# Reordering the turn into the gated MLP: tile 4's attention ahead of the transposes of tiles 0 and 1, tile 3 turned next to tile 2

## The chip, the cores and the metric

The kernel runs on one core of one Trainium2 chip. A core has five engines that run their own instruction queues: TensorE (PE, matrix products, with the loading of weights shown apart as PEld), VectorE (DVE), ScalarE (ACT), GpSimd (POOL) and SyncE (SP), which issues most of the DMA transfers. They meet by semaphores. The metric is device time in microseconds; before the change the median of four runs is 825.15 us (824.64 to 827.29).

## The reference

The program computes the output and the gradients of one transformer layer with S = 2048 rows, D = 640 columns and 32 heads of 20, followed by a gated MLP of width F = 1728. Cut to what matters:

```
phi(t) = where(t > 0, t + 1, exp(t)) + 1e-6
A(x):  q, k, v = heads of x @ wqkv
       kv = phi(k).T @ v ; z = sum of phi(k)          # per head
       o  = (phi(q) @ kv) / (phi(q) . z + 1e-6)
       return o @ wo
B(x):  return (silu(x @ w1) * (x @ w3)) @ w2

h   = x + A(layernorm(x))
out = h + B(layernorm(h))
returns out and, for a given grad_out, the gradients of x, wqkv, wo, w1, w3, w2
```

All inputs and outputs are bf16. The scores are never formed: the attention is linear, so that for one tile of rows it is a product of the normalised phi(q) with one matrix of 640 x 640 that holds kv and wo together (`Wp` in the kernel).

## The kernel before

Rows are worked in 16 tiles of 128 (`t`), and the MLP in four blocks of four tiles (`c`). The order of the work is written by hand: the framework keeps the order in which the program issues instructions on each engine and adds the waits, so a list of steps is the schedule. Every engine takes its own instructions strictly in that order.

The program has these stages: layer norm, q, k, v and the sums over rows for all tiles (to about 74 us); a turn into the second half of the layer (about 74 to 100 us); the forward gated MLP over four blocks with the attention of later tiles mixed in (about 100 to 344 us); then the weight and input gradients (to the end). The change is in the second of these, in the tuple of steps handed to `run` (lines 868 to 876). A step is a function with its arguments. Those that the change moves or passes are:

- `f2_half(t, j, hold)` calls `f2_at` (line 634): half `j` (320 columns) of the attention output of tile `t`, five products into a PSUM buffer named `at`, from the transposed phi(q) of the tile (`pqT`) and `Wp`. For the second halves of tiles 0 to 3 (and both of tiles 5 to 7) a sixth product with the identity adds x (line 640), and ACT copies the sum to `x_sb` (line 647); otherwise DVE adds x (line 649). Then DVE takes the statistics of the half (line 147), and after the second half their aggregate and variance (lines 150 and 153); POOL makes the reciprocal deviation `ln_rs` (line 154). With `hold` the part after the products is kept back until `f2_rest`.
- `f2_hn(t)` (line 727): the normalised rows `hn` of a tile on DVE (line 160), and a store of them issued on SP (line 732). Tiles 0 and 1 have buffers of their own. Tile 2 takes over a buffer of the group `pql`, which held scaled phi(q) of an earlier tile until its DMA transpose (line 376) and its store had read it. Tile 3 takes one of the group `h2`, which held products of tile 6 that the reduction `r_red(6, (0,))` reads.
- `f2_ht(t)` (line 734): for tiles 0 to 3, five transposes of `hn` on PE into a PSUM buffer `trh` (line 744) and one ACT copy of it into `pqT` (line 745), which is then the operand `hnT` of the MLP. For later tiles it is a DMA.
- `mlp_ghh(n)` (line 756): one product of grad_out with w2, five products on PE (line 386) and a cast on ACT (line 406). It needs none of the steps around it.
- `r_red`, `r_inv`, `r_scale`, `r_T` (lines 363 to 376): the denominators of a later tile on DVE, and its DMA transpose on SP.

`trh` and the MLP's and grad_out's products share four PSUM buffers of the group `mm` in turn. The `at` of tile 4 has two buffers of the group `o2` in turn, used before by tiles 0 and 2. The MLP (`mlp`, line 760) follows; its first product reads all four tiles of the first block at once, and so waits for the last of the four copies at line 745.

Of the kernel before, what the change touches and what calls it, by code (L numbers as in the profile page):

```python
# [9 lines left out]
P = 128  # L10
# [8 lines left out]
S, D, H, F = 2048, 640, 32, 1728  # L19
# [36 lines left out]
def kernel(  # L56
# [807 lines left out]
    def kv3():  # L864
# [5 lines left out]
        (f2_wT, 4), (phi_rest,), (q_late, 14), (r_T, 4), (load_x, 4, 6), (r_head, 5), (r_prod, 7),  # L870
        (r_store, 5, 6), (r_store, 4, 5), (f2_m_out,), (q_out, 10, 14), (load_w2T, 8 * P, 10 * P), (mlp_ghh, 4),
        (q_late, 15), (sig_table,), (f2_half, 0, 0), (f2_half, 1, 0), (f2_half, 2, 0), (f2_half, 3, 0), (mlp_ghh, 5),
        (f2_half, 0, 1), (f2_half, 1, 1), (f2_hn, 0), (f2_half, 2, 1), (f2_hn, 1), (f2_half, 3, 1), (f2_ht, 0),
        (f2_half, 4, 0, True), (load_w2T, 10 * P, F), (f2_hn, 2), (f2_ht, 1), (mlp_ghh, 6), (r_red, 6, (0,)),
        (f2_hn, 3), (r_red, 6, (1,)), (f2_ht, 2), (r_inv, 6), (r_scale, 6), (r_T, 6), (mlp_ghh, 7), (f2_ht, 3),
        (f2_half, 4, 1, True), (f2_rest,), (r_red, 7), (r_inv, 7), (r_scale, 7), (r_T, 7), (r_store, 6, 7))
    p1.release()
    pa = pool("pa", "right")

# [627 lines left out]
```

## Time and profile before

| what | us |
|---|---|
| median of 4 runs | 825.15 |
| the profiled execution | 824.92 |
| its span in the trace | 823.20 |
| PE busy | 816.7 (99%) |
| DVE busy | 453.0 (55%) |
| ACT busy | 325.2 (40%) |
| POOL busy | 133.0 (16%) |

Times in the trace count from the start of the span. An instruction's row has its start, its length, engine, line, operation, what it writes and reads, and in brackets the idle time of its engine just before it with what ended that. PE's products are pipelined: a row's length holds the depth of the pipeline, so the next row starts before the last has ended, and a short wait hides in that overlap. Around the edited steps, from 86 to 100 us, PE is busy 12.74 of 14 us, DVE 11.84, ACT 8.52 and POOL 5.36; from 100 to 200 us PE is busy all of the time.

### The profile page before, as it was taken

The numbers are of one execution on the slowest core, as the hardware profiler recorded it, in microseconds if no ns is written. First come the engines' busy times: TensorE is split into PE (matmuls) and PEld (weight loads), VectorE is DVE, ScalarE is ACT, GpSimd is POOL, SyncE is SP. The second block draws the span as 40 slices with busy tenths as digits, with TensorE's granted clock in tenths as the row PEclk, the third lists the DMA queues.
The fourth block names the chain that finished last, engine by engine and source line by source line (L and its number), as shares of the span: only waits on it lengthen the run. The fifth ranks groups of instructions, "written<-read, shape, count | busy, mean of one in ns | idle before, by whom it ended". The sixth has DMA issues, their size and how long they took to land.

```text
span 823.2 us, 14206 instructions
## 1 busy us (share of the span) xinstructions
PE 816.7 (99%) x5549; PEld 522.1 (63%) x5549; DVE 453.0 (55%) x961; ACT 325.2 (40%) x609; POOL 133.0 (16%) x194
## 2 busy tenths in 40 slices
PE   8999999999999999999999999999999999999998
PEld 6677544555555555777777777777777777555554
DVE  7868888999898566300057777772681545200000
ACT  7856688655565666011121212222212334211111
POOL 2243333233322212100001111110220000000000
PEclk9999999999999999999999999999999999999999
DMA  9999989696485556999777898358994898885771
GB/s 223 260 281 228 205 217 298 210 242 166 137 218 156 155 192 167 228 241 266 216 166 182 197 211 185 74 111 173 255 234 93 164 197 178 208 194 140 167 168 38
DMA packets 320883, 157.26 MB, mean 191 GB/s; under 512 B 238704, under 2 KB 314064, under 8 KB 320816
## 3 DMA queue, kind: packets, MB, share of 16 engines
q1 hardware_dynamic: 278768, 115.54, 61.8%
q10 hardware_dynamic: 34720, 16.34, 8.8%
q0 software_dynamic: 7328, 24.48, 8.8%
q8 instruction: 43, 0.70, 0.4%
q14 instruction: 24, 0.20, 0.1%
HBM read 47.01 MB, written 51.13 MB: 119 GB/s over the span
## 4 chain that ended last, share of the span: by engine, by line
PE 96%; DMA 1%; ACT 1%; DVE 1%; issue 0%; SPq 0%; DVEq 0%
PE mm L386 20%; PE job L1271 19%; PE ghn L1070 14%; PE gxn L1429 8%; PE o L833 7%; PE gw L1025 7%; PE big L266 4%; PE gwo L1155 3%; PE macc L416 3%; PE gr L1127 3%; PE dkv L1375 3%; PE at L642 2%; DMA pqT<-pql 1%; DMA wqkv<-in_A_wqkv_dram 1%; PE dkv L1303 1%; PE gp L386 1%
## 5 line engine op out<-in xcount | busy, mean ns | idle before, releaser
L1271 PE MATMUL job<-gb,hnN 128*128 128x432 bf16 (+2 forms) x656 | 117.0, 342 | 0.0
L1070 PEld LDWEIGHTS <-ggb 128*128 128x128 bf16 x864 | 84.4, 98 | 33.0
L1271 PEld LDWEIGHTS <-hnN 128*128 128x128 bf16 x656 | 63.5, 98 | 53.5
L386 PE MATMUL mm<-pqT,w 128*128 128x512 bf16 x405 | 93.6, 379 | 0.3 <-ACT pqT L745 0.3
L386 PEld LDWEIGHTS <-w 128*128 128x128 bf16 x540 | 52.4, 98 | 63.5 <-issue 1.3
L1275 ACT CAST obs<-job 128x432 bf16<-128x432 f32 (+3 forms) x61 | 29.3, 480 | 123.1 <-PE job L1271 123.1
L833 PE MATMUL o<-w,hhT 128*128 128x320 bf16 x448 | 67.7, 299 | 0.0
L1070 PE MATMUL ghn<-w13a,ggb 128*128 128x320 bf16 x448 | 63.5, 299 | 0.0
L1070 PE MATMUL ghn<-w13b,ggb 128*128 128x320 bf16 x416 | 61.4, 299 | 0.0
L386 PE MATMUL mm<-g2T,w2T 128*128 128x512 bf16 x240 | 59.6, 379 | 0.0
L833 PEld LDWEIGHTS <-hhT 128*128 128x128 bf16 x448 | 43.7, 98 | 23.9 <-issue 0.2
L1025 PE MATMUL gw<-g,hb 128*128 128x320 bf16 x416 | 56.8, 299 | 0.0
L1135 POOL TENSOR_TENSOR sz<-Zb,g_h 128x640 f32<-128x640 bf16 x16 | 20.2, 1261 | 198.8 <-DVE g_h L1133 198.8
L1025 PEld LDWEIGHTS <-hb 128*128 128x128 bf16 x416 | 40.5, 98 | 16.1 <-issue 0.3
L1429 PE MATMUL gxn<-wqT,gT 128*128 128x320 bf16 x320 | 48.7, 299 | 0.0
L406 ACT CAST ghh<-mm 128x512 bf16<-128x512 f32 x48 | 28.4, 592 | 44.1 <-PE mm L386 39.3
L772 ACT ACTIVATE sig<-mm 128x512 bf16<-128x512 f32 x56 | 33.7, 601 | 25.1 <-PE mm L386 21.0
L1082 ACT ACTIVATE gs<-ghn 128x640 bf16<-128x640 f32 x16 | 11.2, 703 | 79.0 <-PE ghn L1070 69.2
L386 PEld LDWEIGHTS <-w2T 128*128 128x128 bf16 x260 | 25.2, 98 | 23.6 <-DMA w2T<-in_B_w_dram 0.3
L266 PEld LDWEIGHTS <-pqT 128*128 128x128 bf16 x320 | 30.5, 97 | 14.0 <-issue 1.2
L1429 PEld LDWEIGHTS <-gT 128*128 128x128 bf16 x320 | 31.3, 98 | 12.2
L266 PE MATMUL big<-wqkv,pqT 128*128 128x320 bf16 x250 | 38.5, 299 | 0.2
(210 smaller groups left out, 1282.7 us busy)
## 6 DMA issues: line engine op xcount, KB each, us to landing
hh_d<-hhT SPq DMA_DIRECT2D x24, 256.0 KB, 2.8
gg_d<-gate POOLq DMA_DIRECT2D x24, 256.0 KB, 4.5
gg_d<-ghh POOLq DMA_DIRECT2D x24, 256.0 KB, 3.5
ggb<-gg_d SPq DMA_DIRECT2D x6, 896.0 KB, 5.5
ggb<-gg_d ACTq DMA_DIRECT2D x6, 832.0 KB, 5.9
out_dram<-obs ACTq DMA_DIRECT2D x39, 108.0 KB, 3.1
x_sb<-in_A_x_dram SPq DMA_DIRECT2D x6, 640.0 KB, 6.2
ggb<-gg_d SPq DMA_DIRECT2D x2, 1728.0 KB, 13.3
```

The source lines that it names most:

```text
L266: T.matmul(acc, lhsT=pqT[:, c, t * P:(t + 1) * P], rhs=wqkv[:, c, n0:n0 + HD], start=(c == 0), stop=(c == DT - 1))
L386: T.matmul(acc[:], lhsT=w[:, c, fc * P:(fc + 1) * P], rhs=rhs[:, c, :], start=(c == 0), stop=(c == DT - 1))
L406: A.copy(out=ghh[n // 2][:, n % 2, :], in_=acc[:])
L416: T.matmul(macc[m][j][:, 0:n], lhsT=pk_all[:, t, m * P:(m + 1) * P], rhs=x_ext[:, t, j * HD:j * HD + n], start=(t == 0), stop=(t == ST - 1))
L772: A.activation(sig[:, i, :], gp[:], AF.Sigmoid)
L833: T.matmul(o2["ps"][:, 0:HD], lhsT=hhT[c][:, fc, i * P:(i + 1) * P], rhs=w2[:, fc, j * HD:(j + 1) * HD], start=(fc == 0), stop=(fc == FT - 1))
L1025: T.matmul(acc[:, j, 0:HD], lhsT=hb[b][:, t, i * P:(i + 1) * P], rhs=g2[:, t, j * HD:(j + 1) * HD], start=(t == 0), stop=(t == ST - 1))
L1070: T.matmul(acc[:, j, 0:HD], lhsT=ggb[t // 2][:, k, lo:lo + P], rhs=rhs[:, j * HD:(j + 1) * HD], start=(k == 0), stop=(k == NG - 1))
L1127: T.matmul(gr[t][:, j, 0:HD], lhsT=ghT[t][:, c, :], rhs=wT2[:, c, j * HD:(j + 1) * HD], start=(c == 0), stop=(c == DT - 1))
L1271: T.matmul(acc[:, 0:n], lhsT=lhs[:, t, m * P:(m + 1) * P], rhs=rhs(t), start=(t == 0), stop=(t == ST - 1))
L1275: A.copy(out=ob, in_=acc[:, 0:n])
L1429: T.matmul(acc[:, j, 0:HD], lhsT=g, rhs=wqT[:, k, j * HD:(j + 1) * HD], start=(k == 0), stop=(k == 14))
```

## The change

Only the order of the steps is changed, in one tuple. Tile 4's two halves are issued ahead of the transposes of tile 0 and of tile 1; the first reduction of tile 6 is issued ahead of `hn` of tile 2, and `hn` of tile 3 sooner; the transposes of tile 3 follow those of tile 2; the last grad_out product of the stretch follows them; and the reductions and the scaling of tile 6 stand behind.

```diff
-        (f2_half, 0, 1), (f2_half, 1, 1), (f2_hn, 0), (f2_half, 2, 1), (f2_hn, 1), (f2_half, 3, 1), (f2_ht, 0),
-        (f2_half, 4, 0, True), (load_w2T, 10 * P, F), (f2_hn, 2), (f2_ht, 1), (mlp_ghh, 6), (r_red, 6, (0,)),
-        (f2_hn, 3), (r_red, 6, (1,)), (f2_ht, 2), (r_inv, 6), (r_scale, 6), (r_T, 6), (mlp_ghh, 7), (f2_ht, 3),
-        (f2_half, 4, 1, True), (f2_rest,), (r_red, 7), (r_inv, 7), (r_scale, 7), (r_T, 7), (r_store, 6, 7))
+        (f2_half, 0, 1), (f2_half, 1, 1), (f2_hn, 0), (f2_half, 2, 1), (f2_hn, 1), (f2_half, 3, 1),
+        (f2_half, 4, 0, True), (f2_ht, 0), (load_w2T, 10 * P, F), (r_red, 6, (0,)), (f2_hn, 2), (f2_half, 4, 1, True), (f2_hn, 3),
+        (f2_ht, 1), (mlp_ghh, 6), (r_red, 6, (1,)), (f2_ht, 2), (f2_ht, 3), (r_inv, 6), (r_scale, 6), (r_T, 6),
+        (mlp_ghh, 7), (f2_rest,), (r_red, 7), (r_inv, 7), (r_scale, 7), (r_T, 7), (r_store, 6, 7))
```

Engine by engine, in the order in which the instructions stand:

| engine | before | after |
|---|---|---|
| PE | tile 3's attention, turn 0, tile 4 first half, turn 1, grad_out, turn 2, grad_out, turn 3, tile 4 second half, MLP | tile 3's attention, tile 4 first half, turn 0, tile 4 second half, turn 1, grad_out, turn 2, turn 3, grad_out, MLP |
| DVE | hn 2, reduction, hn 3, reduction | reduction, hn 2, hn 3, reduction |
| ACT | copy 0, copy 1, cast, copy 2, cast, copy 3 | copy 0, copy 1, cast, copy 2, copy 3, cast |
| POOL, SP | | as before |

Here "turn" is the five transposes of a tile, "copy" the ACT copy of them, and "cast" that of a grad_out product.

## The prediction

> **What bounds the kernel now.** I read the page's busy times first, then its chain, then who made TensorE (PE) wait in the whole run, then all engines from 92 to 104 us, where the edited steps run. From the page, busy time of PE and the chain's shares by engine:
>
> ```profile
> PE 816.7 (99%) x5549; PEld 522.1 (63%) x5549; DVE 453.0 (55%) x961; ACT 325.2 (40%) x609; POOL 133.0 (16%) x194
> PE 96%; DMA 1%; ACT 1%; DVE 1%; issue 0%; SPq 0%; DVEq 0%
> ```
>
> PE sets the end. The kernel gets shorter only where PE idles, and PE's waits over the whole run make five lines, 3.1 us together. Two of them belong to the edited stretch:
>
> ```profile
> PE trh L744 <- DVE hn L160: 0.7, 2, 0.5
> ...
> PE mm L386 <- ACT pqT L745: 0.3, 1, 0.3
> ```
>
> The others lie before 91 us. So after 99.8 us nothing is shown to hold PE back, and a shift there should reach the end. The chain in order of time says what the stretch hangs on (start, length, what):
>
> ```profile
> 89.38 6.95 DMA pqT<-pql
> ...
> 96.45 0.46 DVE hn L160
> ...
> 96.95 0.45 PE trh L744 x5
> ...
> 99.01 0.71 ACT pqT L745
> ```
>
> The normalised rows hn of tile 2 take over the buffer of a pql tile, and wait for that tile's transposing DMA, issued at 89.38 and landed at 96.33. Tile 2's transposes, at 96.95, follow from that. The timeline below names POOL as releaser of that hn; but POOL's row for tile 2 ended at 95.29, the one that ended near 96.35 is tile 3's, so I go by the chain. The timeline, PE's rows first, then those of VectorE (DVE) and ScalarE (ACT); the brackets hold idle time and releaser:
>
> ```profile
> 93.76 0.45 PE L744 MATMUL trh<-ident,hn 128*128 128x128 bf16 x5 [0.22 <-DVE hn L160]
> 94.05 0.84 PE L642 MATMUL at<-Wp,pqT 128*128 128x320 bf16 x5
> 94.94 0.45 PE L744 MATMUL trh<-ident,hn 128*128 128x128 bf16 x5
> 95.23 1.24 PE L386 MATMUL mm<-g2T,w2T 128*128 128x512 bf16 x5
> 96.95 0.45 PE L744 MATMUL trh<-ident,hn 128*128 128x128 bf16 x5 [0.48 <-DVE hn L160]
> 97.25 1.24 PE L386 MATMUL mm<-g2T,w2T 128*128 128x512 bf16 x5
> 98.33 0.44 PE L744 MATMUL trh<-ident,hn 128*128 128x128 bf16 x5
> 98.60 0.84 PE L642 MATMUL at<-Wp,pqT 128*128 128x320 bf16 x5
> 99.76 8.79 PE L386 MATMUL mm<-pqT,w 128*128 128x512 bf16 x40 [0.31 <-ACT pqT L745]
> ```
>
> ```profile
> 96.45 0.45 DVE L160 TENSOR_SCALAR hn<-x_sb,ln_mv,ln_rs 128x640 bf16<-128x640 bf16 x1 [0.73 <-POOL ln_rs L154]
> 96.81 0.48 DVE L365 TENSOR_REDUCE rden<-pr 128x16 f32<-128x320 f32 x1
> 97.40 0.45 DVE L160 TENSOR_SCALAR hn<-x_sb,ln_mv,ln_rs 128x640 bf16<-128x640 bf16 x1
> ```
>
> ```profile
> 97.45 0.69 ACT L745 COPY pqT<-trh 128x640 bf16<-128x640 bf16 x1 [0.35 <-PE trh L744]
> 98.53 0.59 ACT L406 CAST ghh<-mm 128x512 bf16<-128x512 f32 x1 [0.39 <-PE mm L386]
> 99.01 0.70 ACT L745 COPY pqT<-trh 128x640 bf16<-128x640 bf16 x1
> ```
>
> The gated MLP's first product (99.76) reads all four tiles of hnT, so it starts when ACT has copied the last transposed tile. That copy (99.01) stood behind the cast of a grad_out product, and tile 3's transposes stood behind that product. Rows overlap by the pipeline's depth, so I count from start to start: five transposes 0.29 us (93.76 to 94.05), five products into at 0.68 (six in 0.81), five into mm 1.08 (97.25 to 98.33). PE's last product of tile 3's attention hands on at 93.38. From there to 99.76 are 6.38 us, with 4 x 0.29 + 2 x 0.68 + 2 x 1.08 = 4.68 of work: 1.70 idle, as 0.38 (before 93.76), 0.21 (94.73 to 94.94), 0.64 (96.31 to 96.95) and 0.48 (99.28 to 99.76).
>
> **The change part by part.** No instruction is added or removed. PE, DVE and ACT change their order inside this stretch; POOL and SP issue the same sequence, so no DMA is moved past another.
>
> *Both halves of tile 4's attention ahead.* The first follows tile 3's attention at once, at 93.38 instead of 94.05. Its PSUM buffer is that of tile 0's second half, copied out at 91.13 + 0.42 = 91.55. Its operand, the transposed tile 4, came by the DMA issued at 86.88 that landed 4.7 us later, at 91.6. It fills the 0.38 wait for tile 0's hn, which is ready at 93.70. Tile 0's transposes run at 94.06 (0.30 later). The second half, behind them, reuses the buffer of tile 2's second half, copied out at 92.76 + 0.42 = 93.18, so it runs from 94.35 to 95.03 and fills the second gap. Tile 1's transposes go to 95.03 (0.09 later), the grad_out product to 95.32, its end to 96.40. Behind these two on PE stand only instructions that would have idled until 96.95 anyway. Cost of the delays: nothing, covered by the DMA that lands at 96.33; were the cover gone, 0.09.
>
> *The reduction ahead of tile 2's hn on DVE.* DVE idles 0.73 us before hn at 96.45. The reduction (0.48) can start at 95.63, 0.07 behind the start of the last ln_ve (95.56), as at 92.36 to 92.43, and ends at 96.11, ahead of the landing. So hn of tile 2 stays at 96.45, and tile 3's follows at the pitch of that row, 0.36, at 96.81 instead of 97.40, 0.59 earlier. Were the DMA to land before 95.6, the reduction would cost hn of tile 2 its 0.36 pitch, most of it beside the grad_out product that lasts to 96.40. Everything behind on DVE moves up by 0.59: the other reduction, tile 6's scaling, the held adds of tile 4 (99.62 to 99.03), the two reductions of tile 7 (101.90 to 101.31).
>
> *Tile 3 next to tile 2 on PE.* Tile 2's transposes stay at 96.95. Tile 3's hn ends at 96.81 + 0.45 = 97.26, PE follows 0.05 later as before, so tile 3's transposes run 97.31 to 97.60 instead of at 98.33. The second grad_out product then fills 97.60 to 98.68.
>
> *The last copy on ACT.* It no longer stands behind a cast. Tile 2's copy starts at 97.45 as before; tile 3's transposes end at 97.31 + 0.44 = 97.75; so it is ACT itself that sets the next start. No row shows two such copies back to back. Lower bound for the pitch: a 128x512 cast, 0.48 (98.53 to 99.01); upper bound: the copy's whole 0.69. The casts last 0.58 to 0.59 and hand on 0.10 before their end, so I take 0.69 - 0.10 = 0.59: start 98.04, end 98.73, and the MLP's first product 0.05 later, at 98.78. With 0.48 PE's own queue decides, 98.68; with 0.69 it is 98.88. The displaced cast now runs about 98.9 to 99.5; its PSUM buffer is wanted by a product near 102 and its result by DVE after 105, so it costs nothing.
>
> *The sum.* 93.38 + 4.68 + idle 0.55 (96.40 to 96.95) + 0.07 + 0.10 = 98.78: 0.98 us earlier, between 0.88 and 1.08.
>
> *What is late next.* ACT's first "up" waits for tile 7's first reduction (102.38 before it, then 102.48). That moves by 0.59 while PE moves by 0.98, so ACT falls 0.39 further behind PE, with "up" at 101.89, done by 102.48. PE's next need of that buffer is its fifth MLP product, at 98.78 + 4 x 1.08 = 103.10: 0.6 us of room. ACT needs four rows at about 0.49, 1.96 per chunk, against PE's 2.16, so it has caught up within two or three chunks. Cost nothing, bounds 0 and 0.39.
>
> The profiled execution took 824.92 (span 823.20 and 1.72 around it), 0.23 under the median 825.15. Less 0.98 that is 823.94, and on the median 824.17: **824.2 us**, 0.12% shorter.
>
> **A page's rule against the trace.** The fourth gap is gone, but transposes now stand together behind an idle 0.55 us: from 96.40 to 97.60 PE does nothing but ten transposes. The row first: five transposes take 0.29, 0.058 each, before and after waits; the granted clock reads 1.00 throughout, but so it does in the slow warm-up at the start, so spacing is the better sign. The Trainium skill ("TensorE: Matmul & The Clock Gate", Part 4) says that transposes do not count as busy for the clock gate, and Part 1 that an idle window of about 3.4 us halves the clock. By the rule 1.2 us is too short to trip it, but the window runs freely; if it tripped, one window at half speed would lose about 1.7 us, an estimate from that page, and the sum would be 0.7 us slower than before, where the rows give 0.98 faster.
>
> **The rivals.**
>
> *Half of it is lost in the stretch.* The landing at 96.33 comes from a busy queue (DMA share 0.9 to 1.4 around it), and hn of tile 2 hangs on it. Each 0.1 us that it lands later moves the whole second half by 0.1, before and after alike; only a landing that differs between the kernels matters, or ACT's 0.39 lag reaching PE. Against it: DMA order is the same. For it: such landings vary (4.7 and 7.0 for two transposes of the same size here). Gain 0.4 to 0.6: about 824.6.
>
> *Nothing reaches the end.* Later a DMA with a fixed start could absorb the shift. Against it: PE shows no wait after 99.8, and later DMAs are released by work that shifts too. Then 825.15.
>
> *Slower: PE loses its full clock.* Place: 96.40 to 97.60, then the MLP's first products. It decides if PE's slow start returns. Its price from this trace: the 34 warm-up products at the start took from 1.12 to 4.72, 3.60 us, where at 0.058 each they would take 1.97; a second such start loses 1.63. Net +0.65: 825.8. Against it: the same stretch held 0.94 us without an ordinary product before (96.31 to 97.25), and the next five took 1.08, full rate. From 0.98 lost on, it is slower than before.
>
> **How the numbers follow.** Full gain 0.62 (own range 823.8 to 824.6); half 0.12; nothing arrives 0.06; clock 0.05; 0.15 for what I do not see, beyond 2.5 us to either side. A measurement of this kernel tells about 0.3%, 2.5 us, from no change, so all four named cases are "same": faster 0.07, same 0.85, slower 0.08, a little more on the slower side because a clock that drops could drop more than once. The range, 823.3 to 825.7, holds the first three cases and the drift of a median between sets of runs (the shown ones span 824.64 to 825.33 but for one at 827.29); the clock case and the unseen are left out.
>
> **What would show it.** Right: tile 4's ten products on PE from 93.4 and 94.35; a reduction of tile 6 on DVE at 95.6, and hn of tiles 2 and 3 some 0.36 apart; tile 3's transposes about 0.36 behind tile 2's; the copy of tile 3 right behind that of tile 2 on ACT; the MLP's first product near 98.8; no new wait on PE after it. Wrong: hn of tile 2 later than 96.5 against the same DMA; the first MLP product still waiting for that copy past 99; a granted clock under 1.00; or an equal start near 98.8 with a PE wait later on that gives it back.

## The result and the profile after

| | before | after |
|---|---|---|
| median, us | 825.02 (54 runs) | 823.93 (35 runs) |
| lowest, us | 824.14 | 823.21 |
| ratio after / before | | 0.9988, 95% 0.9982 to 0.9994 |
| profiled execution, us | 824.92 | 823.88 |
| its span, us | 823.2 | 822.2 |

The kernel is 1.09 us shorter, 0.12% (0.06 to 0.18%). The forecast was 824.2 us, 0.12% shorter. The interval runs from 0.5 to 1.5 us, so that the two agree to 0.1 us is partly luck.

From the page of the kernel after, busy time by engine and the chain's shares by engine. PE works the same 5549 products in 0.5 us less of busy time: a row holds the pipeline's depth, so part of the idle time between products lies inside the rows and counts as busy. Counted from start to start, as below, what went is idle time:

```profile
PE 816.2 (99%) x5549; PEld 522.9 (64%) x5549; DVE 453.2 (55%) x961; ACT 325.7 (40%) x609; POOL 132.6 (16%) x194
PE 95%; DVE 2%; ACT 1%; DMA 1%; SPq 0%; issue 0%; POOL 0%; DVEq 0%; ACTq 0%
```

Who made PE wait in the whole run after the change (total, times, longest). The two lines that belonged to the edited stretch, the 0.7 for `hn` and the 0.3 for the copy, are not there any more, and no line stands in their place; what is left lies before 91 us:

```profile
PE warm L455 <- DVE zero L124: 1.1, 1, 1.1
PE k L266 <- DMA wqkv<-in_A_wqkv_dram: 1.1, 2, 0.7
PE at L642 <- DMA Wp<-pkx: 0.3, 1, 0.3
PE big L266 <- ACT mq L293: 0.2, 1, 0.2
```

PE's timeline after (start, length, what); a row starts before the one above has left the pipeline:

```profile
92.89 0.30 PE L640 MATMUL at<-x_sb,ident 128*128 128x320 bf16 x1
93.03 1.52 PE L642 MATMUL at<-Wp,pqT 128*128 128x320 bf16 x10
94.39 0.44 PE L744 MATMUL trh<-ident,hn 128*128 128x128 bf16 x5
94.67 0.84 PE L642 MATMUL at<-Wp,pqT 128*128 128x320 bf16 x5
95.34 0.44 PE L744 MATMUL trh<-ident,hn 128*128 128x128 bf16 x5
95.62 1.24 PE L386 MATMUL mm<-g2T,w2T 128*128 128x512 bf16 x5
96.86 0.97 PE L744 MATMUL trh<-ident,hn 128*128 128x128 bf16 x10
97.67 1.24 PE L386 MATMUL mm<-g2T,w2T 128*128 128x512 bf16 x5
98.75 5.56 PE L386 MATMUL mm<-pqT,w 128*128 128x512 bf16 x25
```

The two executions have to be laid on each other at the start of the stretch, not at the start of the span: this one came to the stretch 0.33 us later (92.89 here; the same identity product of tile 3 stood at 92.56 before), and 0.27 of that was there at 75 us, ahead of every step that moved. I write D for the time from that identity product to the first product of the gated MLP. D fell from 99.76 - 92.56 = 7.20 to 98.75 - 92.89 = 5.86, by 1.34 us; less the 0.33 that is 1.01, and the span fell by 1.0. Of the idle 1.70 us in the stretch, 0.39 is left: 0.16 (95.62 + 1.08 = 96.70 to 96.86) and 0.23 in the middle of the row of ten transposes (97.15 to 97.38).

The rows of DVE, of POOL and of ACT in the same stretch of the kernel after:

```profile
95.97 0.48 DVE L365 TENSOR_REDUCE rden<-pr 128x16 f32<-128x320 f32 x1
96.36 0.96 DVE L160 TENSOR_SCALAR hn<-x_sb,ln_mv,ln_rs 128x640 bf16<-128x640 bf16 x2
```

```profile
94.94 0.68 POOL L154 TENSOR_TENSOR ln_rs<-ln_ve,mhalf 128x1 f32<-128x1 f32 x1 [0.50 <-DVE ln_ve L153]
96.13 0.71 POOL L154 TENSOR_TENSOR ln_rs<-ln_ve,mhalf 128x1 f32<-128x1 f32 x1 [0.51 <-DVE ln_ve L153]
```

```profile
97.39 1.29 ACT L745 COPY pqT<-trh 128x640 bf16<-128x640 bf16 x2
98.95 0.59 ACT L406 CAST ghh<-mm 128x512 bf16<-128x512 f32 x1 [0.27 <-PE mm L386]
101.96 0.59 ACT L779 CAST up<-mm 128x512 bf16<-128x512 f32 x1 [0.85 <-DVE rden L365]
```

The reduction runs ahead of both `hn`, and `hn` of tile 2 follows at the reduction's pitch (95.97 to 96.36), not at the landing of the DMA, which in this execution came at 89.69 + 6.5 = 96.2; the pitch, 0.39, is the same in a kernel further down in which that `hn` waits for no DMA (95.31 to 95.70). On ACT the two copies stand together, and the cast behind them. The chain in order of time says what held the last transposes:

```profile
95.90 0.17 DVE ln_ve L153
...
96.13 0.72 POOL ln_rs L154
...
96.88 0.46 DVE hn L160
...
97.38 0.45 PE trh L744 x5
97.83 9.71 PE mm L386 x45
```

POOL's reciprocal deviation of tile 3 ends at 96.85, and `hn` of tile 3 starts at 96.88. From the transposes on the chain is PE alone.

### The profile page after: what moved, and what is told of

It is laid out like the page before. It is cut to its first block, busy times and chain, and to the rows that moved or that the text cites. A ratio compares the mean times of both kernels' runs of the same rounds, so it can differ in the third digit from the quotient of the medians.

```text
span 822.2 us, 14206 instructions
## 1 busy us (share of the span) xinstructions
PE 816.2 (99%) x5549; PEld 522.9 (64%) x5549; DVE 453.2 (55%) x961; ACT 325.7 (40%) x609; POOL 132.6 (16%) x194
## 4 chain that ended last, share of the span: by engine, by line
PE 95%; DVE 2%; ACT 1%; DMA 1%; SPq 0%; issue 0%; POOL 0%; DVEq 0%; ACTq 0%
PE mm L386 20%; PE job L1271 19%; PE ghn L1070 14%; PE gxn L1429 8%; PE o L833 7%; PE gw L1025 7%; PE big L266 3%; PE gwo L1155 3%; PE dkv L1375 3%; PE gr L1127 3%; PE macc L416 2%; PE at L642 2%; DMA wqkv<-in_A_wqkv_dram 1%; PE dkv L1303 1%; DVE st L147 1%; DMA Wp<-pkx 1%
```

## The experiments

Two theories. **One chain of several**: PE's work ahead of the MLP is fixed at 4.68 us, and the MLP starts behind the latest of three chains, the `hn` of tile 3 on DVE, the last copy on ACT behind its cast, and whatever PE work is left behind the last transposes; no part of the change shortens all three, so the parts are worth little alone and about 1 us together. **Sum of parts** (the rival): each part fills a gap of its own and brings its share alone. A second rival is that the shift is lost after the stretch.

To compare kernels whose transposing DMA landed at different times, L is the start of `hn` of tile 2 counted from the same identity product. By the first theory D is L plus what must follow: `hn` to transposes 0.50, five transposes 0.29, a grad_out product 1.08, a half of tile 4 0.68, the pitch of two `hn` 0.36 or, with the reduction between them, 0.95.

**Each part alone.** The lines taken out are those of the change's diff; here is what stands in their place, first for the two held halves alone:

```diff
+        (f2_half, 4, 0, True), (f2_ht, 0), (load_w2T, 10 * P, F), (f2_hn, 2), (f2_half, 4, 1, True),
+        (f2_ht, 1), (mlp_ghh, 6), (r_red, 6, (0,)), (f2_hn, 3), (r_red, 6, (1,)),
+        (f2_ht, 2), (r_inv, 6), (r_scale, 6), (r_T, 6), (mlp_ghh, 7), (f2_ht, 3), (f2_rest,),
+        (r_red, 7), (r_inv, 7), (r_scale, 7), (r_T, 7), (r_store, 6, 7))
```

> The held halves of tile 4 alone go ahead of the transposes of tiles 0 and 1; the order of DVE and of tiles 2 and 3 is that of before. Measure: from tile 3's identity product (92.56 in the profile of before, 92.89 in that of after) to the first MLP product; 7.20 us before, 5.86 after. Let L be the start of tile 2's hn counted from the same point (3.89 before, 3.47 after; a DMA landing moves it). Theory A (the parts need each other: PE's work before the MLP is a fixed 4.68 us, and the MLP starts behind whatever chain ends last): the copy of tile 3 still stands behind the cast, so the first MLP product comes at L + 0.50 + 2.80, as before: 6.8 to 7.2, and 0.0 us end to end. The filled gaps only come back as a longer wait for that copy, about 1.1 us instead of 0.48. Theory B (each filled gap counts by itself): 0.38 + 0.21 = 0.59 us less, 6.6, ratio 0.9993.

Measured: 824.68 against 824.72, ratio 1.0003 (0.9994 to 1.0012). PE and then ACT in this kernel:

```profile
98.59 0.44 PE L744 MATMUL trh<-ident,hn 128*128 128x128 bf16 x5
100.02 4.26 PE L386 MATMUL mm<-pqT,w 128*128 128x512 bf16 x19 [0.99 <-ACT pqT L745]
```

```profile
98.79 0.59 ACT L406 CAST ghh<-mm 128x512 bf16<-128x512 f32 x1 [0.37 <-PE mm L386]
99.27 0.70 ACT L745 COPY pqT<-trh 128x640 bf16<-128x640 bf16 x1
```

The gaps ahead of the first transposes are filled, but the copy still stands behind the cast. The half that used to run while PE waited for that copy is gone, so the wait is 0.99 where it was 0.31. Filled at one place, idle again at another.

Tile 3's transposes next to tile 2's, alone:

```diff
+        (f2_ht, 0), (f2_half, 4, 0, True), (load_w2T, 10 * P, F), (f2_hn, 2), (f2_ht, 1),
+        (mlp_ghh, 6), (r_red, 6, (0,)), (f2_hn, 3), (r_red, 6, (1,)), (f2_ht, 2),
+        (f2_ht, 3), (r_inv, 6), (r_scale, 6), (r_T, 6), (mlp_ghh, 7), (f2_half, 4, 1, True), (f2_rest,),
+        (r_red, 7), (r_inv, 7), (r_scale, 7), (r_T, 7), (r_store, 6, 7))
```

> Tile 3's transposes alone go next to tile 2's, the grad_out product behind them; the held halves and DVE's order stay as before. Theory A: tile 3's hn still comes 0.95 us behind tile 2's, so PE idles about 0.66 us between the two turns, and the second held half still stands before the MLP: first MLP product at L + 3.50, 7.0 to 7.4, that is 0.2 us slower than before with the same L. Theory B: the copy is no longer behind the cast, so the 0.48 us gap before the MLP goes: 6.7, ratio 0.9994.

Measured: 824.89 against 824.72, ratio 1.0002 (0.9991 to 1.0013). PE at tile 3's transposes:

```profile
97.67 0.45 PE L744 MATMUL trh<-ident,hn 128*128 128x128 bf16 x5 [0.50 <-DVE hn L160]
```

The copy is out of the way, but tile 3's `hn` is late behind the reduction, and PE waits 0.50 for it between the two turns.

The order on DVE alone:

```diff
+        (f2_ht, 0), (f2_half, 4, 0, True), (load_w2T, 10 * P, F), (r_red, 6, (0,)), (f2_hn, 2),
+        (f2_hn, 3), (f2_ht, 1), (mlp_ghh, 6), (r_red, 6, (1,)), (f2_ht, 2),
+        (r_inv, 6), (r_scale, 6), (r_T, 6), (mlp_ghh, 7), (f2_ht, 3), (f2_half, 4, 1, True), (f2_rest,),
+        (r_red, 7), (r_inv, 7), (r_scale, 7), (r_T, 7), (r_store, 6, 7))
```

> The reduction of tile 6 alone goes ahead of tile 2's hn on DVE; PE and ACT as before. Theory A: tile 3's hn comes 0.5 to 0.6 us earlier but its transposes still stand behind a grad_out product that ends later: nothing, L + 3.30, 6.8 to 7.2, 0.0 us end to end. Theory B (the earlier hn counts by itself): 0.59 us less, 6.6, ratio 0.9993.

Measured: 824.74 against 824.72, ratio 1.0003 (0.9994 to 1.0012). PE in this kernel:

```profile
96.89 1.24 PE L386 MATMUL mm<-g2T,w2T 128*128 128x512 bf16 x5
97.97 0.44 PE L744 MATMUL trh<-ident,hn 128*128 128x128 bf16 x5
```

Tile 3's `hn` is ready early, at 96.91, and its transposes stand behind the grad_out product all the same.

**Two parts.** The held halves and the turn, with the reduction left between the two `hn`:

```diff
+        (f2_half, 4, 0, True), (f2_ht, 0), (load_w2T, 10 * P, F), (f2_hn, 2), (f2_half, 4, 1, True),
+        (f2_ht, 1), (mlp_ghh, 6), (r_red, 6, (0,)), (f2_hn, 3), (r_red, 6, (1,)),
+        (f2_ht, 2), (f2_ht, 3), (r_inv, 6), (r_scale, 6), (r_T, 6), (mlp_ghh, 7), (f2_rest,),
+        (r_red, 7), (r_inv, 7), (r_scale, 7), (r_T, 7), (r_store, 6, 7))
```

> The held halves and tile 3's turn together, DVE's order as before. Theory A: PE idles 0.66 us between the turns of tiles 2 and 3, but nothing of tile 4 is left before the MLP, so the first MLP product follows the grad_out product at L + 2.82: 6.3 to 6.7, 0.48 us faster than before, half of the whole change, ratio 0.9994; the MLP waits for no copy. Theory B (the reduction order is worth nothing, the whole gain is in these two): as after, 5.9 to 6.2, ratio 0.9988.

Measured: 824.10 against 824.72, ratio 0.9993 (0.9985 to 1.0002). PE in this kernel:

```profile
97.14 0.45 PE L744 MATMUL trh<-ident,hn 128*128 128x128 bf16 x5 [0.76 <-DVE hn L160]
98.09 0.45 PE L744 MATMUL trh<-ident,hn 128*128 128x128 bf16 x5 [0.50 <-DVE hn L160]
...
99.46 4.91 PE L386 MATMUL mm<-pqT,w 128*128 128x512 bf16 x22
```

The MLP waits for nothing; both gaps that are left are DVE's. In the stretch this is about half of the whole change (0.48 us at the same landing, table below); the interval of the runs still holds no gain.

The turn and the DVE order, with the held halves as before, run twice on different chips:

```diff
+        (f2_ht, 0), (f2_half, 4, 0, True), (load_w2T, 10 * P, F), (r_red, 6, (0,)), (f2_hn, 2),
+        (f2_hn, 3), (f2_ht, 1), (mlp_ghh, 6), (r_red, 6, (1,)), (f2_ht, 2),
+        (f2_ht, 3), (r_inv, 6), (r_scale, 6), (r_T, 6), (mlp_ghh, 7), (f2_half, 4, 1, True), (f2_rest,),
+        (r_red, 7), (r_inv, 7), (r_scale, 7), (r_T, 7), (r_store, 6, 7))
```

> Tile 3's turn and the reduction order together, without the held halves moved: the second held half stands before the MLP. Same measure and same L as for the first four. Theory A: tile 3's turn comes at L + 0.86, the grad_out product ends at L + 2.23, the held half of 0.68 is PE work behind it, so the first MLP product comes at L + 2.91: 0.39 us faster than before (L + 3.30) at the same L, ratio 0.9995. Theory B (held halves are worth nothing): as after at the same L, L + 2.33, ratio 0.9988.

> Tile 3's turn and the reduction order together once more, without the held halves moved. The profile gave L + 2.91 as worked out, 0.40 us earlier than in the profile of before, the medians no difference (824.62 against 824.58). Theory A: the medians of the first time were moved by late landings of tile 5's transposing DMA (L 4.0 in its profile); a second set lies 0.2 to 0.4 us under before, ratio 0.9996. Rival: the two parts together are worth nothing end to end, ratio 1.0000 or more.

Measured: 824.62 against 824.58, ratio 1.0005 (0.9995 to 1.0014); again 824.96 against 824.84, ratio 1.0001 (0.9993 to 1.0010). PE in the first of the two, and a line of PE's waits in the second:

```profile
96.96 0.81 PE L744 MATMUL trh<-ident,hn 128*128 128x128 bf16 x10 [0.57 <-DVE hn L160]
97.61 1.24 PE L386 MATMUL mm<-g2T,w2T 128*128 128x512 bf16 x5
98.69 0.84 PE L642 MATMUL at<-Wp,pqT 128*128 128x320 bf16 x5
99.36 4.91 PE L386 MATMUL mm<-pqT,w 128*128 128x512 bf16 x22
```

```profile
PE mm L386 <- DMA pqT<-hn: 0.2, 1, 0.2
```

The stretch is as the first theory has it, L + 2.91 in both (0.36 + 0.50 + 0.29 + 1.08 + 0.68), and yet the medians show no gain. In the second profile a part of it went later, at 207.57, where PE waited 0.24 for a transposed `hn`; the first shows no wait of PE on a DMA from 99 to 345 us. So this gain of 0.4 in two profiles is missing from two medians, against the expectation of 0.2 to 0.4 us for the second set. A gain of 0.4 us is a ratio of 0.9995, the lower end of the first interval and inside the second, so the runs neither show it nor exclude it. One profile is one execution: the thirteen profiles of this document reach the stretch at 92.05 to 93.22, and that spread alone is as large as the whole gain.

**The change again**, on one chip with the second set above:

> The changed kernel itself, beside the two others on one chip. Theory A: 1.0 us under before, ratio 0.9988, and 0.2 to 0.7 us over the variants in which tile 2's hn waits for no DMA. Rival (the landing makes no difference to the changed kernel, since the reduction fills that wait): the same as the variant with hn in its own place, ratio 0.9984.

Measured: 823.76 against 824.84, ratio 0.9985 (0.9974 to 0.9995); D = 98.31 - 92.46 = 5.85. The gain is there again; the two expectations, 0.9988 and 0.9984, lie too close for this interval to tell them apart.

Here are all of them beside each other. The last but one column is the gain at the L of the kernel before, 3.89, so with the same landing for all; the last is the difference of the medians from the kernel before on the same chip.

| kernel | L | D in its profile | D by the chains | gain at L = 3.89 | gain, medians |
|---|---|---|---|---|---|
| before | 3.89 | 7.20 | L + 3.30 | 0 | |
| held halves | 3.50 | 6.80 | L + 3.30 | 0 | 0.04 |
| turn | 3.78 | 7.29 | L + 3.50 | -0.20 | -0.17 |
| DVE order | 3.73 | 7.03 | L + 3.30 | 0 | -0.02 |
| held halves, turn | 4.24 | 7.06 | L + 2.82 | 0.48 | 0.62 |
| turn, DVE order | 3.98, 3.68 | 6.89, 6.59 | L + 2.91 | 0.39 | -0.04, -0.12 |
| all three | 3.47, 3.48 | 5.86, 5.85 | L + 2.33, at least 5.86 | 0.97 | 1.09, 1.08 |

All nine D agree with the chains to 0.01 us. Two of them gave terms, the kernel before L + 3.30 and the first profile of the kernel after the floor 5.86; the other seven test them. L + 3.30 is 0.50 + 0.29 + 1.08, then 0.20 to the start of the cast on ACT (98.33 to 98.53 before), 0.48 for the cast and 0.75 for the copy and into PE. L + 2.33 is the forecast's: the second of the two copies starts 0.50 + 0.50 + 0.59 behind `hn` of tile 2, and 0.74 later it is done and handed to PE. No profile of the changed kernel met it, since both had `hn` of tile 2 early; the same two copies in the first profile of turn and DVE order (`hn` at 96.45, copies from 97.45 for 1.29, 0.05 into PE) would give L + 2.34. The floor under "all three", 5.86, is read from the first profile of the kernel after, and its second tests it: POOL's `ln_rs` holds `hn` of tile 3 at 96.88, 3.99 into the stretch, and 0.50 + 0.29 + 1.08 follow. The sum of parts falls: the three alone come to nothing or less in the stretch, each with its new wait in the rows above. The medians alone would not decide it: the rival's 0.9993 lies just outside two of the intervals, and its 0.9994 for the turn inside the third.

**Without the DMA ahead of `hn` of tile 2.** Which row releases that `hn` was read from the chain against the bracket on the row, which named POOL. To settle it, `hn` of tile 2 goes to a place that no DMA holds, the free fifth slot of an older tile, once in the kernel before and once in the kernel after:

```diff
-        hn[t] = (pf.tile([P, D], BF16, name="hn", tag="pql", bufs=4) if t == 2 else
+        hn[t] = (qx[0][:, 4, :] if t == 2 else
```

> The kernel before, with tile 2's hn in a free part of an older tile instead of a buffer of the group pql, so that it waits for no DMA of that group. Theory A (the landing of the transposing DMA holds tile 2's hn, and with it the MLP): L falls to about 3.1, where DVE itself is ready; tile 2's transposes then follow the grad_out product at 3.75, and the first MLP product comes at 6.55, against L + 3.30 with L from 3.5 to 4.2 in the profiles so far (mean 3.8): 0.3 to 0.9, some 0.55 us faster than before, ratio 0.9993. Rival (the bracket is right and POOL's reciprocal deviation holds it, or the landing matters in no typical run): the same as before, ratio 1.0000.

> The changed kernel with tile 2's hn in the same free place. Theory A: the reduction ahead of it holds hn at L = 3.46, tile 3's hn waits for its reciprocal deviation at about 3.97, the first MLP product comes at 5.85 as in the profile of after, where the landing was early; against runs of after whose landing is later (L 3.5 to 4.2) up to 0.7 us faster, some 0.3 in the middle; against before some 1.3 us, ratio 0.9984. Rival (the landing matters in no typical run): as after, ratio 0.9988.

Measured, on one chip: 823.96 for before with its own place, and 823.31 for after with it, against 824.58; ratios 0.9989 (0.9980 to 0.9997) and 0.9984 (0.9976 to 0.9993). DVE, POOL and PE of the first:

```profile
95.14 0.45 DVE L160 TENSOR_SCALAR qx<-x_sb,ln_mv,ln_rs 128x640 bf16<-128x640 bf16 x1
```

```profile
95.29 0.70 POOL L154 TENSOR_TENSOR ln_rs<-ln_ve,mhalf 128x1 f32<-128x1 f32 x1 [0.51 <-DVE ln_ve L153]
```

```profile
95.80 0.44 PE L744 MATMUL trh<-ident,qx 128*128 128x128 bf16 x5
...
98.59 5.77 PE L386 MATMUL mm<-pqT,w 128*128 128x512 bf16 x26 [0.31 <-ACT pqT L745]
```

`hn` of tile 2 starts 3.09 us after the identity product, where it stood at 3.89, without a wait; POOL's row for tile 3 ended later than that, at 95.99. So a DMA that uses the buffer was what held it, and the bracket was wrong. That it was the transposing one shows in the five profiles whose chain holds it, the kernel before among them: its landing moves between 95.97 and 96.51, and `hn` follows each time by 0.12 to 0.13 us (95.97 to 96.10, 96.51 to 96.64). Removing the wait was worth 0.62 us in the kernel before. In the kernel after, the profile with its own place shows what the change has made of that wait: its DMA landed late, and nothing waited for it. The issue to landing of that transpose (a view of line 376; the maximum is this one, issued at 89.15) and the chain:

```profile
DMA to landing us min/median/max: 2.6/3.8/8.1
```

```profile
95.47 0.71 POOL ln_rs L154
...
96.21 0.46 DVE hn L160
96.67 0.05 issue
96.72 0.45 PE trh L744 x5
97.17 9.71 PE mm L386 x45
```

The landing at 89.15 + 8.1 = 97.25 is 1.55 us behind the start of that `hn` (95.70), and D is 5.86 as with a landing in time. The runs of this kernel lie between 823.20 and 824.14. The own place makes the change safe from a late landing; on the medians it is 1.27 under before, against 1.08 and 1.09 for the change itself, too little to tell apart with these intervals. By its mechanism it should be the better kernel of the two; what the runs show is that it beats the kernel before.

**Does a further shift reach the end?** With 0.40 us still idle in the stretch of the changed kernel with its own place (96.04 to 96.20 and 96.48 to 96.72), a half of tile 5's attention is put between the last two turns of that kernel, in place of where it stood in the MLP:

```diff
-        f2_at(t, "o2")
+        f2_at(t, "o2", (1,) if t == 5 else (0, 1))
...
-        (f2_ht, 1), (mlp_ghh, 6), (r_red, 6, (1,)), (f2_ht, 2), (f2_ht, 3), (r_inv, 6), (r_scale, 6), (r_T, 6),
+        (f2_ht, 1), (mlp_ghh, 6), (r_red, 6, (1,)), (f2_ht, 2), (f2_half, 5, 0, True), (f2_ht, 3),
+        (r_inv, 6), (r_scale, 6), (r_T, 6),
```

> As the run before in this list, and the first half of tile 5's attention (six products, 0.81 us of PE) taken from the MLP and put between the turns of tiles 2 and 3, its rest held back like tile 4's. Theory A (PE idles some 0.4 us in the changed kernel, waiting for tile 3's hn and its reciprocal deviation; other work can stand there): the first MLP product comes at about 6.3, but with 0.81 us of work done that came later, so like 5.5: 0.35 us faster than the run before in this list, 1.6 us faster than before, ratio 0.9980. Rival (those products wait for tile 5's transposing DMA, whose landing holds them as it held hn): no gain, or a loss of as much as that landing is late, up to 0.5 us.

Measured: 823.31, the same as without it; ratio 0.9986 (0.9977 to 0.9994). The chain of this kernel, where the later x tiles are loaded:

```profile
112.23 3.55 DMA x_sb<-in_A_x_dram
115.78 0.05 issue
115.83 0.31 PE at L640
```

PE had its work ready at 113.42 + 2.16 = 115.58 and waited 0.25 for this load. The same load ended 0.6 us ahead of its use before the change (113.49 + 3.5, used at 117.57) and just at it after (112.96 + 3.6, used at 116.57). From the first MLP product to the first weight-gradient product PE takes 243.9 us in the kernels before and after (343.7 - 99.76, 342.7 - 98.75) and in six of the nine other profiles with the same work there, 0.2 to 0.4 more in three. This kernel has 0.82 us of work less there, and took 342.1 - 98.58 = 243.5. So it won 0.25 in the stretch (D 6.43, less 0.82 is 5.61, against 5.86) and lost 0.4 behind it, 0.25 of that at this load; where the rest went the profile doesn't name.

The last experiment issues this load earlier, behind the first chunk (128 columns of F) of the MLP instead of the fourth:

```diff
-    r_steps = [{1: ((r4_out, 0, 2),), 2: ((r_load, 8),), 3: ((load_x, 6, 8),), 4: ((r_load, 9), (r4_out, 2, 4)),
+    r_steps = [{0: ((load_x, 6, 8),), 1: ((r4_out, 0, 2),), 2: ((r_load, 8),), 4: ((r_load, 9), (r4_out, 2, 4)),
```

> As the run that moved half of tile 5's attention, and the load of x for tiles 6 and 7 is issued after the first chunk of the MLP instead of the fourth. In the run without this, PE waited 0.26 us at 115.83 for that load, which was issued at 112.2 on SP and landed 3.6 us later. Theory A (that landing took the gain back): tile 6's attention no longer waits, and the end comes 0.2 to 0.35 us earlier than with tile 2's hn in its own place alone: 823.0, ratio to before 0.9981. Rival (another wait takes its place, or the moved load delays the transposing DMAs behind it on SP): no gain, 823.3, ratio 0.9985.

Measured: 823.50 against 824.84, ratio 0.9977 (0.9965 to 0.9989). The load is no longer waited for, and the 0.82 of work stays won: 343.0 - 99.88 = 243.1. But in the profiled execution the half of tile 5 itself met the late DMA (PE's timeline):

```profile
97.83 0.85 PE L642 MATMUL at<-Wp,pqT 128*128 128x320 bf16 x5 [0.58 <-DMA pqT<-pql]
```

It was issued at 89.04 and landed 8.7 us later, so the MLP started late. With the lowest ratio of all and not the lowest median, this kernel is not told apart from the changed kernel with its own place.

## Why the prediction was right, point by point

- **PE sets the end, and its idle time is what can go.** Right. PE's busy time hardly moved, and the shift of the stretch was carried whole: from the first MLP product to the first weight-gradient product it took 243.9 us before and after, and from there to the end of the span 479.5 to 479.6 us in all thirteen profiles. (The five waits of PE add up to 3.2 us as printed, not 3.1.)
- **Both halves of tile 4 ahead cost nothing.** Right. Turn 0 stands 1.50 us behind the identity product (forecast 94.06 - 92.56 = 1.50), turn 1 2.45 (forecast 2.47), the grad_out product 2.73 (forecast 2.76). What I had not said, and the experiments show: alone they bring nothing either, because the second half had been the cover of the last copy.
- **The reduction ahead of `hn` of tile 2.** The order and the early start came as forecast. I had `hn` of tile 2 at the landing in either kernel; in this execution the landing came at 3.3 us of the stretch where it had been 3.77, and the reduction decided, at 3.47. That the landing moves was the ground of the rival "half of it is lost", and here it moved the other way.
- **`hn` of tile 3 0.36 behind.** The one step that was mis-sized, by 0.16: it was 0.52, because POOL's `ln_rs` of tile 3 ended only at 96.85. I had used POOL's end at 96.35 to exclude it as a releaser, and not asked where it stands once the DMA comes earlier. It sets the least D, 5.86; at the forecast's landing it would not have shown.
- **Tile 3's transposes, then the grad_out product.** Right but for that: transposes at 97.38, product 0.29 later, MLP 1.08 behind it.
- **The last copy on ACT, 0.59 behind the one before.** The pitch was right: two copies together took 1.29, less 0.69 is 0.60. The wait of 0.10 that I gave PE for it didn't come, since the later `hn` of tile 3 left ACT time to spare.
- **The sum.** 0.98 forecast; 1.34 in the stretch of the profiled pair, of which the earlier landing made 0.42 (3.89 - 3.47) and the POOL floor took 0.06; 1.09 and 1.08 on the medians. At equal landing the chains give 0.97, but the 2.33 in it is the forecast's own and stands in no profile of the changed kernel.
- **What is late next: ACT's lag costs nothing.** Right: "up" starts 3.21 us behind the first MLP product, where it was 2.72, a lag of 0.49 (forecast 0.39), and PE shows no wait for it.
- **The rivals.** *Half lost*: no, but its ground, the landing, is real: the same transpose landed 5.7 to 8.7 us after issue in these profiles. *Nothing arrives*: no for this change; the mechanism was found one step further, at the load of the later x tiles, which in one profile took back the next 0.25 us. *Clock*: no sign of it. The ten transposes together keep their spacing (0.28 to 0.29 for five), the next products 1.08, and the granted clock is 1.00 in the profile of after. The stretch from 96.70 to 97.67 holds no other product, so the rule of the Trainium skill ("TensorE: Matmul & The Clock Gate", Part 4), that transposes do not count as busy in the way that products do, was put to no test longer than a microsecond.

Open is whether the turn and the DVE order together gain the 0.4 us that two profiles show in the stretch and two medians do not.

## What to carry to other kernels

Where an engine is 99% busy and idles at four places ahead of one meeting point, count every chain that ends at that point before pricing a single gap: filling one only lengthens the wait at the latest chain, and three reorderings that showed no gain alone gave 1.1 us together. Lay two profiles on each other at the first instruction of the edited stretch and write the stretch as a function of whatever in it varies by itself, here one DMA's landing. A buffer taken over from a tile that a DMA still reads brings such a varying term; where another place is free, using that place removes it, and in the kernel before this was worth 0.62 us.

## What the runs showed of the hardware

- The landing of one and the same 128x640 transposing DMA, in the same place of the program, lay between 5.7 and 8.7 us after its issue. Its issue row was 1.25 to 1.35 us long in five of the profiles, with the landing 6.2 to 8.1 us from its start, 2.0 to 2.5 in seven, with the landing 5.7 to 6.5, and 1.75 in the one with 8.7.
- In this stretch POOL's 128x1 reciprocal deviation took 0.55 to 0.56 us where no `hn` ran on DVE beside it for more than its last 0.1 us, and 0.68 to 0.73 where one did: for tile 3 0.55 in the kernel before (95.80 to 96.35, `hn` of tile 2 at 96.45) and 0.71 in the kernel after, where that `hn` runs beside it. A reduction beside it does not do the same: in the DVE order alone it ran to 95.93, beside a deviation from 95.61, which took 0.55. Spans on POOL are rough, but `hn` of tile 3 follows their end by 0.03 us. The Trainium skill ("GPSIMD Engine Reference", "Specifications") says that GpSimd shares its SBUF interfaces with VectorE and contends with some of its instructions; that these rows are such a case fits it, and no run here isolates it.
